# Moving one attention unit and one split past the step at which the accumulators change hands, in a fused recurrence and feed-forward kernel

## The chip, the cores and the metric

The kernel runs on one core of a Trainium2 chip. The metric is the time of one execution on the device, in microseconds; the profile is that of one execution, and its span is counted from the first to the last instruction. The five engines work through their own queues and meet only at semaphores: TensorE (PE, with its weight loads as PEld), VectorE (DVE), ScalarE (ACT), GpSimd (POOL) and SyncE (SP), which issues every DMA of this kernel.

## The reference

A decayed linear recurrence over chunks of 32 tokens feeds a two-layer feed-forward network with softplus. There are 4 batches, 8 heads, 768 tokens per batch, head width 32 and state width 16; the feed-forward network goes from 256 to 2048 and back.

```python
for c in range(nc):                      # chunks of 32 tokens
    ...
    L = np.exp(cum[:, :, :, None] - cum[:, :, None, :]) * causal
    M = np.einsum('bhin,bhjn->bhij', Cc, Bc) * L
    y_intra = np.einsum('bhij,bhjd->bhid', M, xc)
    y_inter = np.einsum('bhin,bhnd->bhid', Cc, state) * np.exp(cum)[:, :, :, None]
    y[:, :, sl] = y_intra + y_inter
    ...
    state = decay_full[:, :, None, None] * state + np.sum(Bx, axis=2)
...
h = x @ w_in
g = np.maximum(h, 0.0) + np.log1p(np.exp(-np.abs(h)))
return (g @ w_out).astype(np.float32)
```

## The kernel before

**Units and steps.** The tokens are cut into 24 units of 128 (6 per batch). Each unit is loaded, scored and turned into rows of the feed-forward input. That input is cut into 6 parts `j` of 512 tokens (4 units each), the inner width into 16 tiles `k` of 128. One *step* is one pair `(j, k)`: `first` makes six matmuls into a bank `hp` (the product with `w_in`, in three terms of a high and a low part, over two halves of the inner sum); `parts_of` makes softplus `e` and its high part `gh` on ScalarE and the low part `gl` on VectorE; `second`, `LAG` = 4 steps later, makes six matmuls into two accumulators `acc0` and `acc1`. Steps 0 to 31 go over parts 0 and 1, eight `k` at a time, steps 32 to 95 over parts 2 to 5.

**Change of accumulators.** Step 36 starts the accumulators of part 2. At step 35 `finish(1)` adds the accumulators of part 1 to an earlier half (`o<-acc,half`, two VectorE instructions, line 793), after which the banks are free, and stores the two results. At a step that begins new accumulators the loop first issues the `hp` matmuls of that step, then the block of `acc`.

**Attention units in the loop.** Up to step 27 the order of all work is written out by hand in a string, `ORDER`. It also holds all stages that split the 64-bit weights into a high and a low part (`W`), the one in which VectorE adds the weights' lowest bits among them (`w<-wraw,w`); that order is fixed. From step 28 on a table `fills` says which unit's work follows which step. For unit `i` with due step `s = 30 + 4 * (i - 12)` it holds:

- `split_whole` (lines 286 and 288, at `s - 4`): the unit's rows of B and C, loaded as `bc`, are masked into `b_rows` (two buffers) and `c_all` or, for even units, `kc` (one place each), by an ACT and a DVE instruction each. Between the two, `lay_apart` issues two DMAs that copy the C rows into `c_rows`, of which there is one.
- `attend_scores` (at `s`): GpSimd makes the decay mask `rm`, TensorE the scores `sp` from `c_rows` and `b_rows`, VectorE weighs them (`m`, line 453) and scales B and C (`bp` line 413, `cc` line 429).
- `prefetch(i + 3)` (at `s + 1`): the DMAs `un` and `bc` of a later unit and, for an even one, two of `gg`. There are four `un` buffers, so unit 16 waits for unit 12's last use; `gg` has two, so unit 16 waits for `y` of the pair 12 and 13.
- for odd `i`: `pair_values` (at `s + 2`), with the matmuls `zp` and `yp` of the pair, and `pair_ends` (at `s + 3`), with the last `yp` matmuls, `y` (line 610) and its two parts `xh` and `xl`.

Within a step the order is: the block of `second`, the block of `first`, the fills.

**What sets the order on each engine.** TensorE's instructions and SP's DMAs are all kept in program order. Those of the other engines are kept in it below step `PINNED` = 31; from there on the scheduler of the framework places them by its own simulated times, also ahead of pinned ones that come earlier in the program. Pinned calls show as the helper's line 125 in the profile, others by their own line; all DMAs show as line 135. In the trace the split of unit 15, planned for step 38, ran at step 34, with its `b_rows` between the two `o` of `finish(1)`.

Of the kernel before, what the change touches and what calls it, by code (L numbers as in the profile page):

```python
# [72 lines left out]
HALF = NFT // 2  # L73
AHEAD = 28
PINNED = 31
LAG = 4
# [26 lines left out]
def recurrence_then_ffn(ctx: ExitStack, tc: tile.TileContext, fst, un, alr, w_in, w_out, const, outT):  # L103
# [795 lines left out]
    def plan(s, f, *args):  # L899
        fills[s].append((f, args))  # L900

    def through(f):
        def run(*args):
            for _ in f(*args):
                pass

        return run

    for i in range(FIRST, NB * NU):
        s = 30 + 4 * (i - FIRST)  # L910
        plan(max(s - 4, AHEAD), split_whole, i)
        plan(s, attend_scores, i)
        plan(s + 1, prefetch, i + 3)
        if i % 2:
            plan(s + 2, through(pair_values), i - 1)
            plan(s + 3, through(pair_ends), i - 1)
# [73 lines left out]
```

## Time and profile before

| | us |
|---|---|
| median of three runs (lowest, highest) | 326.22 (324.23, 327.5) |
| profiled execution | 324.59 |
| its span | 322.9 |
| TensorE busy in the span | 314.8 |
| VectorE busy | 201.9 |
| ScalarE busy | 182.2 |
| GpSimd busy | 38.6 |

A row of a timeline gives the start in us from the start of the span, the duration in us, the engine, the line, the operation, the tile written and those read, the shapes and the number of instructions merged into the row; in brackets stands how long the engine was idle before it and what released it. Buffer numbers are left out of the names, so units are told apart by their order in time. SPq rows are issues of DMAs, not their transfers. A matmul's end is modelled; its start is not, so matmuls are compared by their starts.

### The profile page before, as it was taken

The page shows a single profiled execution, that of the slowest core. Times are in us where ns is not written, and L with a number is a line of the kernel's source. Part 1 is how long each engine was busy: PE and PEld are TensorE (multiplying, and loading weights), DVE is VectorE, ACT ScalarE, POOL GpSimd, SP SyncE. Part 2 cuts the span into 40 slices and gives each one's busy share as a digit, 9 for nine tenths or more (in the row PEclk, how much of TensorE's full clock was granted, in tenths as well). Part 3 has the DMA queues.
Part 4 walks back from the last instruction along what each step waited for, and adds up shares of the span by engine and source line. Part 5 has one row for each costly group of instructions (what it writes and reads, how often), then busy time and mean ns, then how long its engine had stood idle before and what let it go on. Part 6 is the DMA issues. An engine that isn't in the chain of part 4 may idle for free.

```text
span 322.9 us, 5266 instructions
## 1 busy us (share of the span) xinstructions
PE 314.8 (98%) x1968; PEld 255.3 (79%) x1968; DVE 201.9 (63%) x354; ACT 182.2 (56%) x333; POOL 38.6 (12%) x42
## 2 busy tenths in 40 slices
PE   7799999999989999999999999999999999999996
PEld 3568878888868888788888788888888888888885
DVE  5999999887793667874646745776653432322222
ACT  5879878895565665555533834745634344544450
POOL 4661030110200001101202101102100000000000
PEclk9999999999999999999999999999999999999999
DMA  7959748553612145344126236135301000100001
GB/s 258 391 175 374 246 130 225 180 167 108 194 52 82 66 149 146 97 143 119 32 100 162 87 110 155 44 106 154 101 0 35 1 2 0 64 1 2 0 0 66
DMA packets 25178, 36.53 MB, mean 113 GB/s; under 512 B 2112, under 2 KB 13504, under 8 KB 25152
## 3 DMA queue, kind: packets, MB, share of 16 engines
q1 hardware_dynamic: 25152, 36.19, 36.4%
q8 instruction: 15, 0.25, 0.3%
q14 instruction: 11, 0.09, 0.1%
HBM read 28.74 MB, written 3.24 MB: 99 GB/s over the span
## 4 chain that ended last, share of the span: by engine, by line
PE 86%; DVE 6%; DMA 4%; ACT 2%; issue 1%; SPq 1%; ACTq 0%; DVEq 0%
PE hp L125 38%; PE acc L125 37%; PE yp L125 6%; PE sp L125 3%; DMA wraw<-in_w_out 3%; DVE w L125 2%; DMA bc<-in_un 1%; PE zp L125 1%; PE end L125 1%; DVE m L125 1%; ACT signs L125 1%; ACT w L125 1%; DVE wol L125 1%; SPq L135 1%; DVE b_rows L288 0%
## 5 line engine op out<-in xcount | busy, mean ns | idle before, releaser
L722 DVE TENSOR_TENSOR gl<-e,gh 128x512 fp32r<-128x512 f32 x65 | 50.9, 787 | 49.0 <-ACT gh L716 48.7
L125 PE MATMUL hp<-xh,wih 128*128 128x512 f32 (+1 forms) x204 | 77.7, 381 | 0.0
L125 PE MATMUL hp<-xh,wil 128*128 128x512 f32 (+1 forms) x204 | 76.9, 377 | 0.6 <-DVE wil L125 0.6
L125 PE MATMUL hp<-xl,wih 128*128 128x512 f32 (+1 forms) x204 | 76.9, 377 | 0.0
L710 ACT ACTIVATE e<-hp 128x512 f32<-128x512 f32 x65 | 38.7, 595 | 64.8 <-PE hp L125 64.2
L125 PE MATMUL acc<-gh,woh 128*128 128x512 f32 x188 | 74.9, 398 | 0.1
L125 PE MATMUL acc<-gl,woh 128*128 128x512 f32 x188 | 73.5, 391 | 0.0
L125 PE MATMUL acc<-gh,wol 128*128 128x512 f32 x188 | 73.2, 390 | 0.0
L125 PEld LDWEIGHTS hp<-xh,wil 128*128 128x128 f32 x204 | 38.3, 188 | 8.2 <-DVE wil L125 1.1
L125 PEld LDWEIGHTS hp<-xh,wih 128*128 128x128 f32 x204 | 38.4, 188 | 7.7 <-DVE y L125 0.8
L125 PEld LDWEIGHTS hp<-xl,wih 128*128 128x128 f32 x204 | 38.4, 188 | 6.8
L716 ACT CAST gh<-e 128x512 fp32r<-128x512 f32 x65 | 40.2, 618 | 5.1 <-PE acc L125 3.5
L125 PEld LDWEIGHTS acc<-gh,woh 128*128 128x128 f32 x188 | 35.4, 188 | 8.5 <-ACT signs L125 0.8
L125 PEld LDWEIGHTS acc<-gh,wol 128*128 128x128 f32 x188 | 35.3, 188 | 7.5
L125 PEld LDWEIGHTS acc<-gl,woh 128*128 128x128 f32 x188 | 35.4, 188 | 6.5 <-DVE gl L722 0.2
L398 POOL TENSOR_SCALAR_AFFINE_SELECT rm<-fc 128x1024 f32<-128x1024 f32 x11 | 16.2, 1477 | 128.2 <-DVE m L453 96.4
L125 DVE TENSOR_TENSOR gl<-e,gh 128x512 fp32r<-128x512 f32 x31 | 21.2, 687 | 10.9 <-ACT gh L125 10.9
L125 POOL TENSOR_SCALAR_AFFINE_SELECT rm<-fc 128x1024 f32<-128x1024 f32 x13 | 18.7, 1443 | 63.7 <-DVE m L125 53.4
L125 ACT ACTIVATE e<-hp 128x512 f32<-128x512 f32 x31 | 18.0, 592 | 12.5 <-PE hp L125 11.0
L125 ACT CAST gh<-e 128x512 fp32r<-128x512 f32 x31 | 18.6, 616 | 5.6 <-PE acc L125 5.4
L125 DVE TENSOR_TENSOR m<-sp,rm 128x512 f32<-128x512 f32 x26 | 17.2, 682 | 1.8 <-PE sp L125 1.2
L453 DVE TENSOR_TENSOR m<-sp,rm 128x512 f32<-128x512 f32 x22 | 14.1, 684 | 3.8 <-PE sp L125 3.8
(104 smaller groups left out, 313.5 us busy)
## 6 DMA issues: line engine op xcount, KB each, us to landing
bc<-in_un SPq DMA_DIRECT2D x16, 512.0 KB
wraw<-in_w_out SPq DMA_DIRECT2D x8, 512.0 KB
wraw<-in_w_in SPq DMA_DIRECT2D x8, 512.0 KB
un<-in_un SPq DMA_DIRECT2D x16, 256.0 KB
out_t<-o SPq DMA_DIRECT2D x9, 256.0 KB
c_rows<-c_all SPq DMA_DIRECT2D x16, 128.0 KB
gg<-gd SPq DMA_DIRECT2D x16, 128.0 KB
c_rows<-kc SPq DMA_DIRECT2D x16, 128.0 KB
```

Source lines behind the costliest of these rows:

```text
L125: return lambda *a, **k: tc.keep_in_program_order(f(*a, **k))
L135: tc.keep_in_program_order(nc.sync.dma_start(out, in_))
L398: Pl.affine_select(out=rm.rearrange("p h c i -> p (h c) i"), in_=fc[:, u].rearrange("p h c -> p (h c)").unsqueeze(2).broadcast_to([P, NH * ...
L453: V.tensor_tensor(mid[i]["m"][:, 4 * g : 4 * g + 4].rearrange("p h t -> p (h t)"), mid[i].pop(("sp", g)), mid[i]["rm"][:, 4 * g : 4 * g + ...
L710: A.activation(e, h, AF.Softplus)
L716: A.copy(gh, e)
L722: V.tensor_tensor(gl, e, gh.bitcast(F32), op=ALU.subtract)
```

## The change

`halt` is the step that starts the accumulators of part 2: 2 * 8 * 2 + 4 = 36. A unit whose due step `s` lies below `halt` and at most two below it is moved two steps on; that is unit 13 (34 to 36) alone. The split of a unit whose split would fall on `halt - 2` is moved two steps on; that is unit 14's (34 to 36), while its scores stay at 38.

```diff
     for i in range(FIRST, NB * NU):
         s = 30 + 4 * (i - FIRST)
-        plan(max(s - 4, AHEAD), split_whole, i)
+        halt = 2 * HALF * 2 + LAG
+        if s < halt <= s + 2:
+            s += 2
+        plan(s - 2 if s - 4 == halt - 2 else max(s - 4, AHEAD), split_whole, i)
         plan(s, attend_scores, i)
         plan(s + 1, prefetch, i + 3)
```

Every other entry of unit 13 follows its due step. The table of what moves:

| work | step before | step after |
|---|---|---|
| split of unit 13, with its row copies | 30 | 32 |
| scores of unit 13 | 34 | 36 |
| loads of unit 16 | 35 | 37 |
| `zp` and `yp` of the pair 12, 13 | 36 | 38 |
| last `yp`, `y` and its parts of the pair 12, 13 | 37 | 39 |
| split of unit 14, with its row copies | 34 | 36 |

The split of unit 13 leaves the pinned part of the program, which ends below step 31. No instruction is added or removed, and the hand-written order up to step 27 stays, with the weight stages in it.

## The prediction

> **What bounds the kernel now.** I read the page first, then the chain that ended last, then the timeline of each engine between 85 and 180 us, and last the DMA queue's timeline.
>
> ```profile
> span 322.9 us, 5266 instructions
> ...
> PE 314.8 (98%) x1968; PEld 255.3 (79%) x1968; DVE 201.9 (63%) x354; ACT 182.2 (56%) x333; POOL 38.6 (12%) x42
> ...
> PE 86%; DVE 6%; DMA 4%; ACT 2%; issue 1%; SPq 1%; ACTq 0%; DVEq 0%
> ```
>
> TensorE is the bound: it is busy 98% of the span and carries 86% of the chain. From step 28 on the rule is simple: whatever leaves TensorE without work adds to the time, whatever only moves work on another engine adds nothing. The chain gives the unit of the step: six matmuls of `acc`, then six of `hp`.
>
> ```profile
> 146.05 1.36 PE acc L125 x6
> 147.41 1.36 PE hp L125 x6
> ```
>
> A step is 2.72 us. Small groups for the attention units (`sp`, `zp`, `yp`) stand between the steps. The TensorE timeline around step 36, where the accumulators change hands:
>
> ```profile
> 128.96 0.64 PE L125 MATMUL sp<-c_rows,b_rows 128*128 128x256 f32 x4
> 129.44 0.40 PE L125 MATMUL acc<-gh,woh 128*128 128x512 f32 x1
> ...
> 133.54 0.39 PE L125 MATMUL acc<-gh,woh 128*128 128x512 f32 x1
> ...
> 134.51 0.50 PE L125 MATMUL acc<-gh,woh 128*128 128x512 f32 x1
> 134.85 0.40 PE L125 MATMUL acc<-gl,woh 128*128 128x512 f32 x1
> ...
> 135.41 0.43 PE L125 MATMUL zp<-un,bp 128*32 128x64 f32 x16
> ...
> 136.64 0.50 PE L125 MATMUL acc<-gh,woh 128*128 128x512 f32 x1
> ...
> 139.49 0.60 PE L125 MATMUL yp<-cc,tb 128*128 128x128 f32 x4
> ...
> 142.67 0.64 PE L125 MATMUL sp<-c_rows,b_rows 128*128 128x256 f32 x4
> ...
> 154.05 0.64 PE L125 MATMUL sp<-c_rows,b_rows 128*128 128x256 f32 x4
> ```
>
> The `sp` groups are the scores of units 13, 14 and 15 (steps 34, 38, 42); `zp` at 135.41 is the pair of units 12 and 13. The block of step 36 begins at 133.54 and its second accumulator only at 134.51: 1.87 us pass until 135.41 where 1.36 would do. About 0.06 to 0.1 of the excess is the start of a group of small matmuls, as in other pairs, so the halt costs **0.45 us**. What it waited for, on VectorE and GpSimd:
>
> ```profile
> 131.83 0.68 DVE L793 TENSOR_TENSOR o<-acc,half 128x512 f32<-128x512 f32 x1
> 132.43 1.43 DVE L288 SCALAR_TENSOR_TENSOR b_rows<-bc,kb,b_rows 128x512 fp32r<-128x512 f32 x1
> 133.78 0.68 DVE L793 TENSOR_TENSOR o<-acc,half 128x512 f32<-128x512 f32 x1
> ...
> 141.25 0.75 DVE L288 SCALAR_TENSOR_TENSOR kc<-bc,kb,kc 128x512 fp32r<-128x512 f32 x1 [0.22 <-ACT kc L286]
> ...
> 132.05 1.28 POOL L398 TENSOR_SCALAR_AFFINE_SELECT rm<-fc 128x1024 f32<-128x1024 f32 x1 [9.73 <-DVE m L453]
> ```
>
> The second `o`, which frees the second accumulator, stands behind a `b_rows` (unit 15's, pulled forward). That one took 1.43 us while GpSimd made `rm`; the `kc` row, same operation and shape, took 0.75.
>
> **The change, part by part.** (1) Unit 13's scores, with `rm`, two `m`, `bp` and `cc`, go from step 34 to 36, behind the first block of the new accumulators. Two of its effects empty VectorE at the halt: the two `m` come after it, and unit 15's `b_rows`, which needs a buffer that unit 13's `sp` releases, can't run ahead of it. The `rm` which follows `m` moves too. The `o`s then start when the blocks of step 35 are through, about 130 and 131, some 2 us before they are needed: gain **0.45 us**, which is all there is. The same number of instructions runs; `sp` itself (0.48 us, 128.96 to 129.44) only changes place. What is late next there is nothing within 1 us.
>
> The Trainium skill, SBUF — State Buffer, section Who interferes with whom, says that a VectorE instruction with two SBUF inputs and a GpSimd instruction that reads SBUF take turns on a shared port, and the later one waits for the whole of the other. The 1.43 row agrees; by it `rm` holds up VectorE at its new place as well, near 137, by up to 1.3 us. It changes no term here, since `gl` has a cover of about three steps.
>
> (2) Unit 13's split goes from step 30 to 32, out of the part that is pinned to program order (below 31). It costs two ACT and two DVE instructions as before; the scheduler may now pull them forward, as it pulled unit 15's. I take 0; the bad end is a rival below. On SP its two row copies fall behind the loads of unit 15, which then start near 118 instead of 124; the copies are due near 134, so both are covered.
>
> Row copies that ran alone, those of unit 12, and the `sp` that reads them:
>
> ```profile
> 114.31 1.32 SPq L135 DMA_DIRECT2D c_rows<-kc  x2
> ...
> 117.51 0.71 PE L125 MATMUL sp<-c_rows,b_rows 128*128 128x256 f32 x4
> ```
>
> (3) Unit 14's split and its row copies to 36. They write the one `c_rows` that unit 13's `sp` reads, so they can start only when that ends. With 0.48 less ahead of it, step 36 begins at 133.06; `sp` of unit 13 ends at 133.06 + 1.36 + 0.48 = 134.9. The copies are needed by the `sp` of unit 14 after four blocks (5.44), `zp` and `yp` (1.23, 135.41 to 136.64): 141.6. That leaves 6.7 us. Alone, such copies took 3.2 (issue 114.31 to `sp` 117.51). Cost 0, with 3.5 us to spare.
>
> (4) The pair 12/13 from 36 and 37 to 38 and 39, the loads of unit 16 from 35 to 37. This is where I expect a price. SP's queue is in program order: `un` 16, `bc` 16, `gg` 16 (step 37), then the row copies of unit 15 (38), then the loads of unit 17 (39). Step and place of unit 15's copies stay, what stands ahead of them gets later.
>
> ```profile
> 136.33 0.34 SPq L135 DMA_DIRECT2D un<-in_un  x1
> 136.72 0.42 SPq L135 DMA_DIRECT2D bc<-in_un  x1
> ...
> 143.34 2.03 SPq L135 DMA_DIRECT2D c_rows<-c_all  x2
> ...
> 161.01 0.33 SPq L135 DMA_DIRECT2D un<-in_un  x1
> 161.44 0.38 SPq L135 DMA_DIRECT2D bc<-in_un  x1
> 168.88 1.19 SPq L135 DMA_DIRECT2D gg<-gd  x2
> 170.18 1.36 SPq L135 DMA_DIRECT2D c_rows<-c_all  x2
> ```
>
> ```profile
> 164.63 0.60 PE L125 MATMUL yp<-cc,tb 128*128 128x128 f32 x4
> ```
>
> ```profile
> 140.49 0.72 ACT L286 ACTIVATE kc<-bc,kb 128x512 fp32r<-128x512 f32 x1 [0.20 <-DMA bc<-in_un]
> ...
> 166.74 0.72 ACT L286 ACTIVATE kc<-bc,kb 128x512 fp32r<-128x512 f32 x1 [5.30 <-DMA bc<-in_un]
> ...
> 178.09 0.72 ACT L286 ACTIVATE c_all<-bc,kb 128x512 fp32r<-128x512 f32 x1 [5.61 <-DMA bc<-in_un]
> ```
>
> ```profile
> 140.13 0.69 DVE L610 TENSOR_TENSOR y<-yp,gg 128x512 f32<-128x512 f32 x1 [0.76 <-PE yp L125]
> ...
> 167.50 0.75 DVE L288 SCALAR_TENSOR_TENSOR kc<-bc,kb,kc 128x512 fp32r<-128x512 f32 x1 [3.12 <-ACT kc L286]
> 168.17 0.68 DVE L610 TENSOR_TENSOR y<-yp,gg 128x512 f32<-128x512 f32 x1
> ```
>
> `un` 16 waits for the matmuls of the pair, 0.92 us after `zp` starts (135.41 to 136.33); `gg` 16 waits for `y` of the pair. In the new order `zp` starts at 134.9 + 5.44 = 140.3, `un` 16 at 141.3, `bc` 16 at 141.7; the last `yp` read starts at 140.3 + 1.23 + 0.48 + 2.72 = 144.8, 3.5 to 3.6 us behind `un` 16. Which of `y` and unit 16's `kc` does VectorE take first? Before, with 3.16 us between (136.33 to 139.49), `y` went first; in the next pair, with 3.62 (161.01 to 164.63), `kc` went first and held `y` until `bc` had landed. The new distance is nearly the second, so I take `kc` first. From the issue of `bc` to ACT's `kc` took 3.77 us (136.72 to 140.49) or 5.30 (161.44 to 166.74): 145.5 to 147.0. From there over `kc`, `y` and `gg` to the first row copy took 3.44 (166.74 to 170.18): 148.9 to 150.4, against 143.34 before. These copies land, from the first issue, in no less than 3.2 us (unit 12's) and no more than 7.9 (170.18 to 178.09, when the `bc` load behind them had landed too). With `gg` just ahead and loads just behind they share the engines, so I take the middle, 5.5: 154.4 to 155.9. TensorE wants unit 15's `sp` at 154.05 - 0.45 = 153.6. It stands **0.8 to 2.3 us, I take 1.55**; it is in order, so that is lost whole. With 7.9 the loss would be 4.7; with 3.2 and the early landing nothing.
>
> By the DMA: Bandwidth & Descriptors page of the Trainium skill, section Anatomy of one DMA, a transfer takes about 2.0 us and its bytes at 436 GB/s, an estimate of 3.0 for two copies of 128 KB issued 0.66 apart. Unit 12's 3.2 agrees; by it alone nothing would be lost at 153.6. Its form is measured for another issuing path, and no row here shows it for copies between other loads.
>
> ACT and VectorE stand up to 5.3 us for `bc`, as at 166.74; there TensorE kept its pace, because `e`, `gh` and `gl` run four steps ahead. I cost this at 0.
>
> **Sum.** -0.45 + 1.55 = **+1.1 us**. Against the profiled execution, 324.59 us (span 322.9), that is 325.7. The profiled one lies 1.63 below the median 326.22 of the three runs (324.23 to 327.5). The four times average 325.6, so I give **326.7** for a median.
>
> **The rivals.** (A) The row copies of unit 15 are in time: `y` goes first, as in the pair before, or they land in 3.2 to 3.6. With `y` first, `gg` follows at 146.2, the copies at 147.5, landed by 153.0 even with 5.5. Then only the gain is left: -0.45, 325.2 on the same average. For it: the first pair. Against: the distance of 3.6.
>
> (B) Slower: unit 13's split, unpinned, is pulled ahead of the weight stages, and ACT stands on `bc` 13.
>
> ```profile
> 85.92 0.34 SPq L135 DMA_DIRECT2D bc<-in_un  x1
> ...
> 88.62 0.62 ACT L125 CAST wih<-w 128x512 fp32r<-128x512 f32 x1
> ...
> 90.87 0.50 PE L125 MATMUL hp<-xh,wil 128*128 128x512 f32 x1 [0.63 <-DVE wil L125]
> ```
>
> `bc` 13 is issued at 85.92 and lands 3.77 to 5.30 later, at 89.7 to 91.2. If its `c_all` stands in ACT ahead of `wih` (88.62), `wih` starts 0.72 after the landing, 1.8 to 3.3 late, and TensorE, which already waits for `wil` at 90.87, loses as much: +2.9 to +4.4 with the stall, or +1.4 to +2.9 without. It decides only if the scheduler takes `bc` 13 as landed before 88.6. Against it: the load goes out less than 3 us before.
>
> (C) The change doesn't do what it says: other work takes VectorE ahead of `o`, or the stall and the gain cancel: 0, 325.6.
>
> **How the numbers follow.** Stall 0.50; (A) 0.32; (B) 0.09; (C) 0.09. About 1%, 3.2 us, is what a measurement of this kernel can tell from no change. All but the upper end of (B) and a stall by the 7.9 lie within; medians of runs that spread by 3.3 us add a little on both sides: faster 0.03, same 0.89, slower 0.08. The range takes (A) with 0.9 us for the spread below, 324.3, and the worst usual stall above (325.6 - 0.45 + 2.3 and about 1.1 of spread): 328.6.
>
> **What would show it.** Right for (1): no gap between the two accumulators at step 36, both `o` done before the block. Right for (4): `kc` 16 before `y` on VectorE, unit 15's row copies issued after 148.5, and TensorE idle ahead of the third `sp` from here. (A): copies at 147.5 or earlier and no gap. (B): an ACT wait for `bc` near 88 to 91. Wrong altogether: a gap at unit 14's `sp`, or a different order of work before 110 us.

## The result, and the profile after

The changed kernel is slower by 0.8%: 328.69 us median of 20 runs (326.48 to 331.83) against 326.57 us for the kernel before (324.23 to 329.7, 20 runs), ratio 1.0081 with a 95% interval of 1.0056 to 1.0106, or 1.8 to 3.5 us. The ratio is that of the means with the one run of each twenty left out that was in the chip's slow state, so it is not the ratio of the two medians. The forecast was 326.7 (+1.1 us) with a range up to 328.6. The time lies just above that range, and the loss, 2.6 us by the ratio, was more than twice the one forecast.

From the page of the changed kernel, the span, and the chain that ended last by engine and by line:

```profile
span 327.0 us, 5262 instructions
...
PE 91%; DMA 5%; DVE 2%; ACT 1%; SPq 0%; issue 0%; DVEq 0%
PE acc L125 39%; PE hp L125 39%; PE yp L125 6%; PE sp L125 4%; DMA wraw<-in_w_in 2%; DMA c_rows<-c_all 2%; DMA bc<-in_un 1%; PE zp L125 1%; PE end L125 1%; PE gp L125 1%; DVE w L125 0%; PE fp L125 0%; DVE gl L125 0%; SPq L135 0%; ACT logs L125 0%
```

The instruction counts of TensorE, VectorE, ScalarE and GpSimd are those of before (1968, 354, 333, 42). New in the chain is `c_rows<-c_all`, 2% of the span; the page of before has no such entry. Row copies of an odd unit now carry time. TensorE's timeline from the change of accumulators on:

```profile
135.30 0.39 PE L125 MATMUL acc<-gh,woh 128*128 128x512 f32 x1
...
135.98 0.39 PE L125 MATMUL acc<-gh,woh 128*128 128x512 f32 x1
...
136.66 0.64 PE L125 MATMUL sp<-c_rows,b_rows 128*128 128x256 f32 x4
...
142.69 0.43 PE L125 MATMUL zp<-un,bp 128*32 128x64 f32 x16
...
143.92 0.74 PE L125 MATMUL sp<-c_rows,b_rows 128*128 128x256 f32 x4
...
147.25 0.60 PE L125 MATMUL yp<-cc,tb 128*128 128x128 f32 x4
```

```profile
157.98 0.71 PE L125 MATMUL sp<-c_rows,b_rows 128*128 128x256 f32 x4 [1.95 <-DMA c_rows<-c_all]
```

The first two rows are the two accumulators of step 36: the second begins 0.68 us after the first, as three matmuls take, and the block ends at 136.66, 1.36 after it began. The halt is gone. On VectorE the two `o` now stand side by side and are through at 135.02:

```profile
133.74 1.28 DVE L793 TENSOR_TENSOR o<-acc,half 128x512 f32<-128x512 f32 x2
```

The third `sp` is unit 15's; it waits for its row copies. SP's issues, ScalarE and VectorE show why:

```profile
143.62 0.34 SPq L135 DMA_DIRECT2D un<-in_un  x1
144.05 0.38 SPq L135 DMA_DIRECT2D bc<-in_un  x1
149.80 1.19 SPq L135 DMA_DIRECT2D gg<-gd  x2
151.10 1.37 SPq L135 DMA_DIRECT2D c_rows<-c_all  x2
152.52 0.59 SPq L135 DMA_DIRECT2D un<-in_un  x1
```

```profile
147.66 0.72 ACT L286 ACTIVATE kc<-bc,kb 128x512 fp32r<-128x512 f32 x1 [3.62 <-DMA bc<-in_un]
```

```profile
148.42 0.75 DVE L288 SCALAR_TENSOR_TENSOR kc<-bc,kb,kc 128x512 fp32r<-128x512 f32 x1 [1.92 <-ACT kc L286]
149.09 0.68 DVE L610 TENSOR_TENSOR y<-yp,gg 128x512 f32<-128x512 f32 x1
```

This is the forecast chain link by link: `un` 16 goes out 0.93 us behind `zp`, VectorE takes `kc` first and waits for `bc`, then come `y`, `gg` and the copies. They go out at 151.10 and `sp` starts at 157.98, 6.9 us later.

A second loss was not forecast. VectorE's and TensorE's timelines some 25 us before the `sp` of unit 12 (119.74), in the changed kernel:

```profile
92.98 0.27 DVE L125 SCALAR_TENSOR_TENSOR state<-state,fr,zp 128x64 f32<-128x64 f32 x1
93.19 0.75 DVE L288 SCALAR_TENSOR_TENSOR c_all<-bc,kb,c_all 128x512 fp32r<-128x512 f32 x1
93.86 0.42 DVE L125 TENSOR_TENSOR tb<-state,kb 128x256 f32<-128x256 f32 x1
94.20 0.28 DVE L125 TENSOR_TENSOR cc<-un,fr 128x128 f32<-128x128 f32 x1
```

```profile
94.54 0.71 PE L125 MATMUL yp<-cc,tb 128*128 128x128 f32 x4 [0.83 <-DVE cc L125]
```

And before the change, the same place on VectorE and TensorE:

```profile
91.34 0.27 DVE L125 SCALAR_TENSOR_TENSOR state<-state,fr,zp 128x64 f32<-128x64 f32 x1
91.64 0.42 DVE L125 TENSOR_TENSOR tb<-state,kb 128x256 f32<-128x256 f32 x1
```

```profile
92.33 0.71 PE L125 MATMUL yp<-cc,tb 128*128 128x128 f32 x4 [0.26 <-DVE cc L125]
```

Unit 13's `c_all`, no longer pinned, stands between `state` and `tb` of a pair whose `yp` TensorE is waiting for. From `state` to `tb` it is 0.88 us instead of 0.30, and TensorE's wait grew from 0.26 to 0.83 us.

**Two stretches.** Single spans can't be compared to within a microsecond here (last section). Two stretches of TensorE's timeline can: P runs from the `sp` of unit 11 to that of unit 12, Q from there to that of unit 15. Their ends, before (117.51 and 154.05 stand in the prediction):

```profile
84.63 0.64 PE L125 MATMUL sp<-c_rows,b_rows 128*128 128x256 f32 x4
```

and in the changed kernel, besides 157.98:

```profile
86.28 0.64 PE L125 MATMUL sp<-c_rows,b_rows 128*128 128x256 f32 x4
```

```profile
119.74 0.71 PE L125 MATMUL sp<-c_rows,b_rows 128*128 128x256 f32 x4
```

So P went from 32.88 to 33.46 (+0.58) and Q from 36.54 to 38.24 (+1.70). From there to the end it is 168.85 and 169.02 (+0.17). Together that is +2.45, within the interval of the runs (+2.6 by the ratio).

### The profile page after: what moved, and what is told of

The parts are those of the page before. It is cut to its first block, busy times and chain, and to the rows that moved or that the text cites. A ratio compares the mean times of both kernels' runs of the same rounds, so it can differ in the third digit from the quotient of the medians.

```text
span 327.0 us, 5262 instructions
## 1 busy us (share of the span) xinstructions
PE 316.5 (97%) x1968; PEld 256.2 (78%) x1968; DVE 201.1 (61%) x354; ACT 182.1 (56%) x333; POOL 38.4 (12%) x42
## 4 chain that ended last, share of the span: by engine, by line
PE 91%; DMA 5%; DVE 2%; ACT 1%; SPq 0%; issue 0%; DVEq 0%
PE acc L125 39%; PE hp L125 39%; PE yp L125 6%; PE sp L125 4%; DMA wraw<-in_w_in 2%; DMA c_rows<-c_all 2%; DMA bc<-in_un 1%; PE zp L125 1%; PE end L125 1%; PE gp L125 1%; DVE w L125 0%; PE fp L125 0%; DVE gl L125 0%; SPq L135 0%; ACT logs L125 0%
## 5 line engine op out<-in xcount | busy, mean ns | idle before, releaser
L722 DVE TENSOR_TENSOR gl<-e,gh 128x512 fp32r<-128x512 f32 x65 | 49.8, 771 | 51.1 <-ACT gh L716 50.3
L125 DVE TENSOR_TENSOR gl<-e,gh 128x512 fp32r<-128x512 f32 x31 | 21.2, 686 | 10.7 <-ACT gh L125 10.7
```

The costliest lines, as they stand in the source:

```text
L125: return lambda *a, **k: tc.keep_in_program_order(f(*a, **k))
L722: V.tensor_tensor(gl, e, gh.bitcast(F32), op=ALU.subtract)
```

## The experiments

| kernel | P | Q | ratio to before (95% interval) |
|---|---|---|---|
| before | 32.88 | 36.54 | 1 |
| changed | 33.46 | 38.24 | 1.0081 (1.0056 to 1.0106) |
| e1: changed, split 13 at 30 | 32.92 | 37.82 | 1.0064 (1.0025 to 1.0102) |
| e2: changed, `gg` 16 behind the row copies | 33.30 | 36.09 | 1.0000 (0.9979 to 1.0021) |
| e3: both edits | 32.75 | 36.11 | 0.9976 (0.9948 to 1.0004) |
| e4: before, split 13 at 32 | 33.47 | 37.20 | 1.0042 (1.0010 to 1.0073) |
| e5: before, pair two steps later | 32.90 | 38.14 | 1.0064 (1.0034 to 1.0094) |
| e6: changed, loads of 17 later | 33.49 | 36.80 | 1.0015 (0.9983 to 1.0046) |
| e7: changed, split 16 in order | 33.30 | 36.46 | 1.0036 (0.9998 to 1.0073) |
| e8: before, split 15 in order | 32.72 | 36.17 | 0.9987 (0.9952 to 1.0022) |

P and Q are in us, from the starts of the `sp` rows of one profiled execution each. P falls into two groups: 33.30 to 33.49 in the five kernels with unit 13's split at step 32, 32.72 to 32.92 in the five with it at step 30.

**e1, the split of unit 13 back in the pinned part.**

```diff
-        plan(s - 2 if s - 4 == halt - 2 else max(s - 4, AHEAD), split_whole, i)
+        plan(30 if i == 13 else s - 2 if s - 4 == halt - 2 else max(s - 4, AHEAD), split_whole, i)
```

> The change, with unit 13's split back at step 30, where it is pinned to program order. Two stretches of TensorE's timeline are compared: P, from the sp of unit 11 to the sp of unit 12 (32.88 us before, 33.46 in the changed kernel), and Q, from the sp of unit 12 to that of unit 15 (36.54 and 38.24). Theory: the extra time of P is unit 13's c_all, which VectorE took ahead of the state, tb and cc of the last hand-ordered pair; so P goes back to 32.9 and Q stays at 38.2 with the gap ahead of unit 15's sp; ratio to before about 1.006. Rival (P's extra is chance of one execution, the whole loss sits in Q): P stays within 0.1 of what chance gives, ratio about 1.008. Rival (the loss comes from the freedom of the split, not from the queue): Q falls to 36.1 and the ratio below 1.001.

P fell to 32.92, as the theory says, and the gap ahead of unit 15's `sp` stayed (Q 37.82, 0.4 less than in the changed kernel, as the copies were a little faster: 151.55 to 157.97). In all five kernels with the split at step 32 `c_all` stands between `state` and `tb` and `yp` waits 0.83 or 0.84 us; in the other five it does not, and `yp` waits 0.26 to 0.28. The split's freedom costs the 0.5 us of P and does not make the gap.

**e2, `gg` of unit 16 behind unit 15's row copies.**

```diff
-            if i % 2 == 0:
+            if i % 2 == 0 and i != 16:
                 load_growth(i)
...
     plan(AHEAD, prefetch, FIRST + 2)
+    plan(38, load_growth, 16)
```

> The change, with the two gg loads of unit 16 issued behind the row copies of unit 15 instead of ahead of them. Theory: the copies then wait only for unit 14's sp, are issued some 0.2 us behind it instead of 7 us, land before they are wanted, and the gap of about 2.1 us ahead of unit 15's sp is gone: Q 36.1, P 33.5, ratio to before about 1.000. Rival (the pair of units and unit 14's sp in one step cost TensorE the time, through VectorE or the banks, and the late copies only coincide): Q stays near 38 and the ratio near 1.008.

The copies now go out right behind unit 14's `sp` (143.04), and unit 15's `sp` waits for nothing:

```profile
143.82 1.26 SPq L135 DMA_DIRECT2D c_rows<-c_all  x2
149.58 1.18 SPq L135 DMA_DIRECT2D gg<-gd  x2
```

```profile
154.99 0.64 PE L125 MATMUL sp<-c_rows,b_rows 128*128 128x256 f32 x4
```

Q is 36.09, 2.15 below the changed kernel and 0.45 below the kernel before. The pair and unit 14's `sp` still share step 38, so that rival is out: without the two `gg` ahead of the copies in SP's queue there is no loss. What made it as large as it was, e6 and e7 ask.

**e3, both edits.** The diffs are those of e1 and e2.

> Both edits together: unit 13's split at step 30 and gg of unit 16 behind unit 15's row copies. Theory: only the gain at the change of accumulators is left: P 32.9, Q 36.1, ratio to before 0.9987 (0.42 us). Rival (the halt's 0.45 us comes back elsewhere): Q 36.5, ratio 1.000. Rival (the pair in one step with unit 14's sp costs time): Q 37 or more.

P 32.75 and Q 36.11: only the gain of the halt is left. 0.9976 is the lowest ratio of the study; its interval reaches to 1.0004, so a gain is likely and not proved by the times. The stretches say 0.13 + 0.43 us, and the 0.13 is no more than the scatter of P among kernels with the split at step 30.

**e4, the split of unit 13 alone.**

```diff
-        plan(max(s - 4, AHEAD), split_whole, i)
+        plan(32 if i == 13 else max(s - 4, AHEAD), split_whole, i)
```

> The kernel before with one edit: unit 13's split at step 32, nothing else moved. Theory: the split is free to run early, its c_all stands on VectorE ahead of the pair's state, P 33.5, Q 36.5 with the halt of 0.45 as before; ratio 1.0018. Rival (P's extra is chance): P 32.9, ratio 1.000. Rival (unit 13's copies, behind unit 15's loads on SP, come late for its sp at step 34): Q above 37.

P is 33.47 as expected, but Q grew too, by 0.66, by a way none of the theories had. It lies above the 37 of the last rival, but not for that rival's reason: unit 13's `sp` was on time, 11.47 us after unit 12's (11.45 before). Unit 13's row copies now stand behind the loads of unit 15, and unit 15's `c_all` must wait until they have been read out of its one place, 8.5 us after their issue at 121.43. ScalarE, VectorE, and the second accumulator of step 36 on TensorE:

```profile
129.93 0.72 ACT L286 ACTIVATE c_all<-bc,kb 128x512 fp32r<-128x512 f32 x1 [4.64 <-DMA c_rows<-c_all]
```

```profile
133.59 1.28 DVE L453 TENSOR_TENSOR m<-sp,rm 128x512 f32<-128x512 f32 x2
134.78 0.68 DVE L793 TENSOR_TENSOR o<-acc,half 128x512 f32<-128x512 f32 x1
135.38 1.43 DVE L288 SCALAR_TENSOR_TENSOR b_rows<-bc,kb,b_rows 128x512 fp32r<-128x512 f32 x1
136.73 0.68 DVE L793 TENSOR_TENSOR o<-acc,half 128x512 f32<-128x512 f32 x1
```

```profile
137.46 0.50 PE L125 MATMUL acc<-gh,woh 128*128 128x512 f32 x1 [0.76 <-DVE o L793]
```

ScalarE stood 4.64 us; `c_all`, `gl` and the `m` behind them came later on VectorE, and with them both `o`. The halt became longer: the second accumulator begins 1.60 us after the first (135.86), against 0.97 before. In the changed kernel the same wait is there (4.33 us) and costs nothing: without the `m` ahead of them and `b_rows` between them both `o` are through at 135.02, just before the block at 135.30.

**e5, the pair alone.**

```diff
         plan(s, attend_scores, i)
+        if i == 13:
+            s += 2
         plan(s + 1, prefetch, i + 3)
```

> The kernel before with the pair of units 12 and 13 and the loads of unit 16 two steps later; unit 13's scores and its split stay at 34 and 30, unit 14's split at 34. Theory: the loss hangs on the pair alone, since un 16 and gg 16 wait for it and unit 15's row copies stand behind them on SP; the halt of 0.45 us stays. Q (from unit 12's sp to unit 15's sp, 36.54 us before, 38.24 in the changed kernel, 37.82 with the early split) comes to 38.2 to 38.6, P to 32.9, ratio to before about 1.006. Rival (the moved scores of unit 13 make the copies late): Q 36.5, ratio 1.000.

```profile
156.56 0.71 PE L125 MATMUL sp<-c_rows,b_rows 128*128 128x256 f32 x4 [1.51 <-DMA c_rows<-c_all]
```

Q is 38.14 with unit 13's scores where they were, and the halt is still in it (0.91 us between the two accumulators). The loss comes from the pair of units 12 and 13 and the loads of unit 16, which this edit moves together, and not from unit 13's scores.

**e6, nothing behind the copies.**

```diff
-        plan(s + 1, prefetch, i + 3)
+        if i != 14:
+            plan(s + 1, prefetch, i + 3)
...
     plan(AHEAD, prefetch, FIRST + 2)
+    plan(42, prefetch, 17)
```

> The change, with the loads of unit 17 behind the row copies of unit 16, so that nothing follows unit 15's row copies for some us; gg stays ahead of them. It asks why these copies took 6.9 us from the first issue to unit 15's sp (151.10 to 157.98) where unit 12's took 3.2. Theory: the loads issued right behind (768 KB) share the DMA engines; without them the copies land within about 4.2 us of the first issue, before the sp is wanted, and Q falls to 36.1 to 36.3. Rival (the gg loads just ahead cost the time): 5.5 us or more remain, with a gap of 0.7 us or more ahead of the sp and Q at 36.8 or above.

```profile
148.09 1.19 SPq L135 DMA_DIRECT2D gg<-gd  x2
149.39 1.37 SPq L135 DMA_DIRECT2D c_rows<-c_all  x2
```

```profile
154.68 0.71 PE L125 MATMUL sp<-c_rows,b_rows 128*128 128x256 f32 x4 [0.55 <-DMA c_rows<-c_all]
```

SP's next issue comes at 155.42. A miss for the theory as it was put: without the loads behind, the copies still took 5.3 us (149.39 to 154.68), not 4.2, and Q is the 36.80 of the rival. Of the 3.7 us by which they were slower than unit 12's, 1.6 went with the loads behind them; the rest stayed, with two `gg` loads just ahead.

The traces also hold the packets in which the DMA engines move the data: 512 bytes each for the row copies, 1 KB for `gg`, 2 KB for `un`, 4 KB for `bc` (size times number gives the bytes of each transfer).

| row copies | their packets | us | other data packets in that time |
|---|---|---|---|
| unit 12, before | 115.61 to 117.04 | 1.4 | none; `un` behind begins at 117.05 |
| unit 15, e6 | 150.68 to 153.74 | 3.1 | `gg` until 152.87 |
| unit 15, changed | 152.40 to 156.73 | 4.3 | `gg` until 155.49, `un` from 153.85, `bc` from 154.91 |

So `gg` shared the engines with the copies behind it. Unit 12's copies had `un`, `bc` and `gg` issued behind them too (115.72 to 116.86), as close as unit 15's, but those began to move only when the copies were through. In the changed kernel, with `gg` ahead, the same loads came while the copies still ran.

**e7, unit 16's split in program order.** `split_whole` keeps its instructions in order for `i == 16`:

```diff
     def split_whole(i):
+        was, in_order[0] = in_order[0], in_order[0] or i == 16
         stages = split_unit(i)
...
+        in_order[0] = was
```

> The change, with unit 16's split kept in program order, so that VectorE takes y of the pair 12 and 13 ahead of unit 16's kc. Theory: kc, waiting for bc 16, held y, gg and the row copies by about 1.2 us; y starts 0.6 us after the last yp read, the first row copy goes out about 7.2 us after zp of the pair instead of 8.4 (142.69 to 151.10), and with copies as slow as before a gap of about 0.9 us is left: Q 37.0, ratio about 1.004. Rival (the copies' own time matters, not who goes first): Q stays within 0.3 of 38.2. Rival (the order was all of it): Q 36.1.

VectorE takes `y` (line 612 in this file) as soon as `yp` is done, and the copies go out 1.2 us earlier against `zp`:

```profile
146.24 0.69 DVE L612 TENSOR_TENSOR y<-yp,gg 128x512 f32<-128x512 f32 x1 [1.25 <-PE yp L125]
```

```profile
148.26 1.37 SPq L135 DMA_DIRECT2D c_rows<-c_all  x2
```

```profile
154.56 0.71 PE L125 MATMUL sp<-c_rows,b_rows 128*128 128x256 f32 x4 [0.18 <-DMA c_rows<-c_all]
```

Q is 36.46. The copies took 6.3 us here instead of 6.9, so the gap came out at 0.37 (36.46 - 36.09) rather than 0.9. Who goes first on VectorE was worth 1.2 of the 2.15 us; another 0.6 came from the faster copies.

**e8, the halt without moving a unit.** The edit is that of e7, in the kernel before and for `i == 15`.

> The kernel before with one edit: unit 15's split kept in program order, so that its b_rows can't stand between the two o at the change of accumulators; no unit moves. Theory: the halt was that b_rows and the rm that held it; both o are through before the second accumulator is wanted, Q falls from 36.54 to 36.1, P stays 32.9, ratio 0.9987. Rival (the two m of unit 13 ahead of the o are enough to cause the halt): a gap of 0.2 us or more stays and Q is 36.4 or above. Rival (unit 15's row copies come late now that its c_all is): a gap ahead of unit 15's sp.

```profile
134.41 0.68 DVE L795 TENSOR_TENSOR o<-acc,half 128x512 f32<-128x512 f32 x1
135.01 1.42 DVE L724 TENSOR_TENSOR gl<-e,gh 128x512 fp32r<-128x512 f32 x1
136.36 0.68 DVE L795 TENSOR_TENSOR o<-acc,half 128x512 f32<-128x512 f32 x1
```

```profile
137.28 0.39 PE L125 MATMUL acc<-gh,woh 128*128 128x512 f32 x1
...
137.96 0.39 PE L125 MATMUL acc<-gh,woh 128*128 128x512 f32 x1
```

No gap, and Q is 36.17, 0.37 below the kernel before, with the two `m` still ahead of the `o`. But the theory's reason does not hold. A `gl` now stands between the two `o` and is held up by `rm` as `b_rows` was (1.42 us against 1.43), and the second `o` starts 1.95 us after the first in both kernels. What changed is the first `o`: it starts 2.87 us ahead of its block, and 1.71 before (131.83 to 133.54). The edit also took unit 15's `c_all` from its place ahead of the `m`. Before:

```profile
129.97 0.75 DVE L288 SCALAR_TENSOR_TENSOR c_all<-bc,kb,c_all 128x512 fp32r<-128x512 f32 x1 [1.55 <-ACT c_all L286]
130.63 1.28 DVE L453 TENSOR_TENSOR m<-sp,rm 128x512 f32<-128x512 f32 x2
```

and here:

```profile
133.21 1.29 DVE L455 TENSOR_TENSOR m<-sp,rm 128x512 f32<-128x512 f32 x2 [1.04 <-PE sp L125]
```

Before, the `m` began 1.67 us after their `sp` (128.96), since VectorE stood for ScalarE's half of `c_all`, which stood for the load of `bc`. Here they begin 0.51 us after it (132.70). These 1.16 us are the whole shift of the `o`: the second is done at 137.04, 0.92 us before the second accumulator at 137.96. Two more kernels fit: in e5 the `m` begin 1.61 us after their `sp` and the accumulators lie 0.91 apart, in e4 it is 2.31 and 1.60, and before it is 1.67 and 0.97. So in these kernels the halt follows the delay of the `m` behind unit 15's `c_all`. No run here takes only `b_rows` or only the `m` out of the way.

The ratio, 0.9987, is the forecast one; at this size the times can't tell it from 1, the stretch can.

## Why the prediction was wrong

**Step 1, the halt: the size right, the reason in part.** -0.45 forecast; Q of e2 and e3, where nothing else is left, is 0.45 and 0.43 below before. Some of that match is luck: e8 has no gap at the halt either and gains 0.37, so 0.06 to 0.08 of it came with the move in another way, which no run isolates. The two effects named, `m` and `b_rows`, did leave the place, but unit 15's `c_all` ahead of the `m` was not named, and e8 shows that without its delay the `m` ahead of the `o` and 1.4 us of other work between them make no gap. That `c_all` also explains the margin: in the changed kernel the `o` start at 133.74, 1.6 us ahead of their blocks, and are done 0.9 us ahead, not some 2.

**Step 2, unit 13's split: wrong.** It was priced at 0, with a rival in which ScalarE stands on `bc` 13. The split was indeed pulled forward, but `bc` had landed. What it cost was VectorE's time: one `c_all` of 0.75 us on a chain from `wil` over `state`, `tb` and `cc` to `yp` that TensorE was already waiting for. P grew by 0.58 in the changed kernel, 0.59 in e4, and 0.04 with the split back at 30 (e1). The row that would have shown it was in the trace of before: `yp` waited 0.26 us for `cc`. An instruction that counts as free costs most of its length when it lands on a waited-for chain, here 0.58 of 0.75.

**Step 3, unit 14's copies: right.** Its `sp` stands right behind `yp` at 143.92.

**Step 4, unit 15's copies: the mechanism right, the size wrong.** Order on SP, `kc` ahead of `y`, and a gap ahead of unit 15's `sp` came as forecast, and the chain from ScalarE's `kc` to the first copy took 3.44 us (147.66 to 151.10), exactly the row used. `bc` landed earlier than assumed (3.61 us to ScalarE's `kc` against a middle of 4.5), which alone would have made the gap 0.6. The copies themselves were mis-sized: 5.5 taken as the middle between 3.2 and 7.9, 6.9 measured. The 3.2 came from copies that the prediction calls alone; loads had been issued right behind them, but what they lacked was a `gg` ahead (e6). The gap was 2.15 us (Q, 38.24 against 36.09) instead of 1.55.

**The sum.** -0.45 + 0 + 1.55 = +1.1 forecast; -0.45 + 0.58 + 2.15 = +2.3 measured in the stretches. About half of the miss is step 2, half the size in step 4. There is a third error, in the base. The forecast stood on 325.6, the average of four times of the kernel before, and twenty runs of it have a median of 326.57. So of the 2.0 us between 326.7 and 328.69 about 1.0 is the base and about 1.0 the change, by the medians. The time is only 0.1 above the range: with step 2's 0.58 in the sum, or with the right base, it would have been inside.

The estimate of 3.0 us from the Trainium skill, DMA: Bandwidth & Descriptors, section Anatomy of one DMA, holds for unit 12's copies, whose packets moved alone (3.2); for copies between other loads the runs show 5.3 to 8.5, and the measurement decides. By the same page of the Trainium skill, section Why a DMA increments its semaphore by 16 and not by 1, a transfer counts as landed only when the last of its engines is done. A share of each engine taken by other transfers would then lengthen the whole; the packets agree, with 1.4 us alone, 3.1 beside `gg` and 4.3 beside `gg` and the loads behind.

Of the remaining 2.1 us (5.3 - 3.2), 1.6 lie in the packets, with `gg` as the only other data on the engines; the rest lies between the last packet and `sp` (0.94 us in e6, 0.47 for unit 12), and its cause stays open.

## What to carry to other kernels

When work is moved in a kernel whose DMAs leave one queue in program order, list what stands in that queue behind each transfer whose trigger gets later: here the scores and the pair that moved lost nothing at their new places, and the copies of unit 15, which did not move, lost 2 us. When an instruction leaves a part pinned to program order, look for the waits in the trace of before that it can now fall into, and price it at its own length there. A transfer in company took about twice what it took alone here (5.3 to 6.9 us against 3.2, and 8.5 in e4), so a deadline should be checked against a row that has the same neighbours, those ahead in the queue above all. And a halt that one instruction seems to make by standing in the way may be decided by another one earlier on that engine: compare when the first of the group starts, and not only what stands inside it.

## What was not expected of the hardware

**The start varies by more than the change.** Up to the `sp` of unit 11 all the kernels run the same program, yet in the ten profiles it came between 84.39 us (e6) and 88.53 (e8). The windows of the first 20 us show the granted TensorE clock (the last but two of the columns); before the change, and in e8:

```profile
0.00:20.00 20.00, 15.99 (x144) 10.03 (x144) 16.07 (x35) 14.07 (x35) 10.96 (x23) 1.00 0.81 283
```

```profile
0.00:20.00 20.00, 16.36 (x88) 11.07 (x90) 12.76 (x28) 12.10 (x29) 8.78 (x21) 0.74 0.80 281
```

1.00 and 84.63 us, 0.74 and 88.53 us. It is not the clock alone: e6 had 0.91 there and the earliest `sp`, e1 had 0.91 too and 87.23. All of it arises early: from the first `sp` made from `c_rows`, at 49.23 (e6) to 53.37 us (e8), to that of unit 11 it is 35.16 us in all ten. Its cause stays open. This is why 4.1 us lie between the two profiled spans (322.9 and 327.0), 1.65 of them ahead of unit 11's `sp`, and only 2.6 between the kernels by their ratio.

**GpSimd's `rm` held up VectorE at its new place too.** In the changed kernel it moved with the `m`, and met unit 15's `b_rows` again, in another place:

```profile
138.58 1.61 POOL L398 TENSOR_SCALAR_AFFINE_SELECT rm<-fc 128x1024 f32<-128x1024 f32 x1 [14.02 <-DVE m L453]
```

```profile
138.97 1.75 DVE L288 SCALAR_TENSOR_TENSOR b_rows<-bc,kb,b_rows 128x512 fp32r<-128x512 f32 x1
```

1.75 us against 0.75 for the `kc` of the same shape. The prediction had expected this of a `gl`, and that it costs nothing; the latter is so, as no gap on TensorE follows.
